# One set of hand-written instruction orders for another in a fused long-convolution and token-MLP kernel

## The chip, the core and the metric

The kernel runs on one core of one Trainium2 chip. The time is that of one execution on the device, in microseconds (us), from repeated runs of the same program; lower is better. The core has five engines, each with its own queue of instructions that it works through in order: TensorE (PE in the profile; PEld is its loading of weights), VectorE (DVE), ScalarE (ACT), GpSimd (POOL) and SyncE (SP, which here only issues DMAs). Engines wait for each other on semaphores.

## The reference, cut to what matters

All tensors are bf16. S = 2048 positions, D = 448 channels, F = 1792.

```python
def _A_ref(q, k, v, shift_k, ssm_k, ssm_D):
    # k_shift: a causal convolution of k with 4 taps (shift_k)
    kv = k_shift * v
    # y: a causal convolution of kv with the filter ssm_k, over all 2048 positions, by FFTs of length 4096
    y = y + kv * ssm_D[None, None, :]
    return q * y

def _B_ref(x, w1, b1, w2, b2):
    h = _layernorm(x, axis=-1)
    u = jnp.einsum("bsd,sf->bdf", h, w1) + b1
    u = _gelu(u)
    y = jnp.einsum("bdf,fs->bds", u, w2) + b2
    return (lambda x, *d: x.transpose(*d))(y, 0, 2, 1)

x = A_q
h = x + _A_ref(_layernorm(x, axis=-1), A_k, A_v, A_shift_k, A_ssm_k, A_ssm_D)
h2 = h + _B_ref(_layernorm(h, axis=-1), B_w1, B_b1, B_w2, B_b2)
return h2
```

So: a short convolution of k, times v; a long convolution with the filter; a gate by the normalised x; then a normalisation and an MLP that mixes positions.

## The kernel before, in words

Position s is written as 16 q + r: q is the partition (128 of them), r one of 16 **row blocks**. The long convolution is a Fourier transform in two stages of matmuls, a product, and two inverse stages. The work is written as steps; each has a name, and the number behind the dot counts the parts of a step, the number behind the colon the instructions of a part (`k1.8:0-7` are eight matmuls, `k1.8:8` what follows them). All line numbers are those of the kernel before.

- `tables` makes the sine tables on the chip: iotas and small products on GpSimd, phases on VectorE (L837 to L844, two halves `tables.6` and `tables.5`), the sine on ScalarE (L847). `tables.4` are small integer sums on VectorE (L822 to L831); `tables.7` makes the tables of the second stage (GpSimd L854, L858, L871; ScalarE L862).
- `loads`, `xload`: DMAs of the filter, k, v and x on SyncE.
- `kT` transposes the filter on TensorE (L1037) and `kv.1` to `kv.8` transpose k (L965); VectorE or ScalarE copies each result out of PSUM (L741 on VectorE, L738 on ScalarE). `kv.9` to `kv.16` are the short convolution on TensorE (L991) and the product with v on VectorE (L1006).
- `k1` and `u1` are the first stage for the filter and for kv (L1058), 16 parts each; every part has an evacuation of 128x896 out of PSUM by ScalarE or VectorE (L1066, L1068), and every second one three DMAs that shuffle partitions, two on GpSimd and one on SyncE (L1074).
- `k2` and `u2` are the second stage (L1093), 16 parts of four matmuls each, and an evacuation for each pair half (L738, L739, L741, L742). A part of `k2` reads what the shuffles of four parts of `k1` wrote: `k2.12` those of `k1.1`, `k1.5`, `k1.9` and `k1.13`.
- `i1` are the products on VectorE (L1160, 16 of them, `i1.15:0` the last), the first inverse stage on TensorE (L1177), evacuations, and copies to the place of the second inverse stage (L1188 and L1201, "inverse copies"; those of row blocks 14 and 15 are separate small ones). `ct0` and `ct` transpose sine tables (L1107) for the second inverse stage.
- `q` and `xn` are the statistics of x (L1237 and L1239 on VectorE, the inverse root on GpSimd) and the normalised x of the first four row blocks (L1270, L1272).
- `i2` is the second inverse stage, one row block r after another (L1303, L1309), then the gate (L1319 on ScalarE, L1321 on VectorE), the product with x (L1329, L1339), sums of squares (L1357), the inverse root on GpSimd (L1367 to L1381) and the normalised row block Q (L1388).
- `mlp`: L1435 and L1445 accumulate w1 over the 16 row blocks of Q for 14 groups of features, seven of them in PSUM while row blocks still come; L1425 is the gelu; L1457 multiplies by w2, and L1460 adds and writes.

What sets the order: five strings, one per engine, list all instructions, and a sixth gives each use of PSUM its bank. Nothing else decides. The scheduler only walks these lists to find out who has to wait for whom:

```python
ORDER = {
    "pe": (
...
        for token in ORDER[e].split():
            step, _, span = token.partition(":")
            lo, _, hi = span.partition("-")
            for k in range(int(lo), int(hi or lo) + 1):
                q.append(steps[step][k])
```

An engine whose next instruction waits does nothing in the meantime, whatever stands behind it.

Of the kernel before, what the change touches and what calls it, by code (L numbers as in the profile page):

```python
# [36 lines left out]
    ),  # L37
    "act": (
# [9 lines left out]
    ),  # L48
    "dve": (
# [14 lines left out]
    ),  # L64
    "pool": (
# [14 lines left out]
    ),  # L80
# [1439 lines left out]
```

## Time and profile before

| what | value |
|---|---|
| time, median of 3 runs (lowest, highest) | 170.63 us (170.56, 170.69) |
| the profiled execution: its own time, its span | 170.65 us, 168.8 us |
| TensorE clock granted in it | 1.000 |
| GpSimd busy | 58.4 us |
| DMA moved | 35.15 MB, mean 208 GB/s |

The span runs from the first to the last instruction of the profiled execution; 1.85 us of its time lie outside. "Busy" counts the time in which an engine executes; matmuls overlap each other, and a busy TensorE is not TensorE at its peak. A row of a timeline gives start, length, engine, line, operation, output and input, count, and in brackets how long the engine was idle ahead of it and what ended that. A row by stretches gives the stretch and its length, then for each engine the busy time and the number of instructions.

### The profile page before, as it was taken

The page shows a single profiled execution, that of the slowest core. Times are in us where ns is not written, and L with a number is a line of the kernel's source. Part 1 is how long each engine was busy: PE and PEld are TensorE (multiplying, and loading weights), DVE is VectorE, ACT ScalarE, POOL GpSimd, SP SyncE. Part 2 cuts the span into 40 slices and gives each one's busy share as a digit, 9 for nine tenths or more (in the row PEclk, how much of TensorE's full clock was granted, in tenths as well). Part 3 has the DMA queues.
Part 4 walks back from the last instruction along what each step waited for, and adds up shares of the span by engine and source line. Part 5 has one row for each costly group of instructions (what it writes and reads, how often), then busy time and mean ns, then how long its engine had stood idle before and what let it go on. Part 6 is the DMA issues. An engine that isn't in the chain of part 4 may idle for free.

```text
span 168.8 us, 3562 instructions
## 1 busy us (share of the span) xinstructions
PE 160.0 (95%) x1416; PEld 93.3 (55%) x1416; DVE 101.9 (60%) x191; ACT 90.4 (54%) x130; POOL 58.4 (35%) x155
## 2 busy tenths in 40 slices
PE   6999999989899989879999999999999999999994
PEld 2787755453333333334554555555577777777783
DVE  7988999999999999999987440000003213132231
ACT  3599848979999999999685803103550000000000
POOL 8345727694830555675777330000000000000000
DMA  5999898893758766748999999930000111101111
GB/s 161 407 308 385 270 290 327 329 362 126 222 134 318 248 195 186 208 135 273 388 398 403 424 420 422 415 129 0 0 0 9 50 54 54 54 2 56 54 54 54
DMA packets 15564, 35.15 MB, mean 208 GB/s; under 512 B 3804, under 2 KB 9644, under 8 KB 15548
## 3 DMA queue, kind: packets, MB, share of 16 engines
q1 hardware_dynamic: 12396, 28.26, 46.1%
q0 software_dynamic: 3008, 6.58, 12.1%
q8 instruction: 11, 0.18, 0.5%
q10 hardware_dynamic: 144, 0.08, 0.2%
q14 instruction: 5, 0.04, 0.1%
HBM read 22.05 MB, written 1.84 MB: 141 GB/s over the span
## 4 chain that ended last, share of the span: by engine, by line
PE 70%; ACT 14%; DMA 5%; DVE 5%; issue 2%; POOL 2%; SPq 0%; DVEq 0%; ACTq 0%
PE ps L1457 25%; PE ps L1435 13%; PE ps L1445 13%; ACT arena L738 7%; DMA arena<-arena 5%; ACT arena L739 4%; PE ps L1309 3%; PE ps L965 3%; ACT arena L1068 3%; PE ps L1024 3%; PE ps L1058 3%; PE ps L1037 3%; DVE arena L1160 2%; POOL arena L1074 2%; PE ps L991 2%
## 5 line engine op out<-in xcount | busy, mean ns | idle before, releaser
L1460 DVE SCALAR_TENSOR_TENSOR arena<-ps,arena 128x448 bf16<-128x448 f32 (+2 forms) x17 | 11.1, 656 | 55.8 <-PE ps L1457 55.8
L1457 PE MATMUL ps<-arena 128*128 128x448 bf16 (+2 forms) x238 | 42.7, 342 | 0.0
L1457 PEld LDWEIGHTS ps<-arena 128*128 128x128 bf16 x238 | 33.3, 145 | 9.5
L1435 PE MATMUL ps<-arena 128*128 128x448 bf16 x112 | 23.5, 353 | 0.0
L738 ACT CAST arena<-ps 128x896 bf16<-128x896 f32 (+1 forms) x29 | 23.1, 933 | 0.0
L1068 ACT CAST arena<-ps 128x896 bf16<-128x896 f32 x24 | 20.2, 919 | 4.1 <-PE ps L1058 3.6
L1445 PE MATMUL ps<-arena 128*128 128x448 bf16 x112 | 22.3, 352 | 0.0
L1074 POOL DMA_DIRECT2D arena<-arena x32 | 17.6, 556 | 7.9 <-ACT arena L1068 7.7
L1425 ACT ACTIVATE arena<-ps,arena 128x448 bf16<-128x448 f32 x14 | 8.2, 632 | 19.3 <-PE ps L1445 10.3
L1093 PE MATMUL ps<-arena 128*64 128x448 bf16 x128 | 15.3, 361 | 1.8 <-ACT arena L739 0.9
L1435 PEld LDWEIGHTS ps<-arena 128*128 128x128 bf16 x112 | 10.7, 98 | 10.6 <-DVE arena L1388 1.1
L1445 PEld LDWEIGHTS ps<-arena 128*128 128x128 bf16 x112 | 11.0, 98 | 10.2
L1160 DVE TENSOR_TENSOR arena<-arena 128x1792 bf16<-128x1792 bf16 x16 | 16.5, 1083 | 0.0
L1177 PE MATMUL ps<-arena 64*128 64x448 bf16 x128 | 14.1, 351 | 1.1 <-ACT arena L738 0.5
L1058 PE MATMUL ps<-arena 128*32 128x448 bf16 x256 | 14.5, 355 | 0.5 <-ACT arena L1068 0.3
L1201 POOL DMA_DIRECT2D arena<-arena x16 | 9.3, 585 | 13.9 <-ACT arena L738 13.0
L1093 PEld LDWEIGHTS ps<-arena 128*64 128x64 f16 x128 | 5.5, 108 | 10.7 <-ACT arena L739 3.4
L1177 PEld LDWEIGHTS ps<-arena 64*128 64x128 f16 x128 | 5.2, 94 | 9.8 <-DVE arena L1160 3.1
L1388 DVE TENSOR_SCALAR arena<-arena 128x448 bf16<-128x448 f32 x16 | 7.6, 509 | 4.8 <-POOL arena L1381 4.8
L1058 PEld LDWEIGHTS ps<-arena 128*32 128x32 f16 x256 | 5.2, 95 | 7.7 <-ACT arena L1068 2.6
L1237 DVE BATCH_NORM_STATS2 arena<-arena 128x6 f32<-128x448 bf16 x16 | 9.4, 613 | 0.0
L739 ACT ACTIVATE arena<-ps 128x896 bf16<-128x896 f32 x10 | 8.6, 926 | 1.1 <-PE ps L1093 1.1
(99 smaller groups left out, 190.4 us busy)
## 6 DMA issues: line engine op xcount, KB each, us to landing
arena<-in_B_w_dram SPq DMA_DIRECT2D x8, 896.0 KB, 9.9
arena<-in_B_w_dram SPq DMA_DIRECT2D x2, 2048.0 KB, 17.3
arena<-arena SPq DMA_DIRECT2D x16, 224.0 KB, 3.8
arena<-arena POOLq DMA_DIRECT2D x32, 112.0 KB, 3.6
arena<-in_B_w_dram SPq DMA_DIRECT2D x2, 1536.0 KB, 18.8
arena<-arena POOLq DMA_DIRECT2D x13, 196.0 KB, 3.8
arena<-in_A_k_dram SPq DMA_DIRECT2D x4, 448.0 KB, 5.8
arena<-in_A_v_dram SPq DMA_DIRECT2D x4, 448.0 KB, 9.2
```

Source lines behind the costliest of these rows:

```text
L738: return e.copy(out=dst(), in_=src())
L739: return e.activation(out=dst(), in_=src(), func=ACT.Copy, scale=scale)
L1058: op("pe", lambda e, W, b=b, r=r, q=q, x=x, c0=c0: e.matmul(PS[32 * q:32 * q + 32, b.slots[x], 0:D], E[:, 2 * r + x, c0:c0 + 32], src[:, r ...
L1068: return e.copy(out=dst, in_=Ppair(b)) if W == "act" else e.tensor_copy(out=dst, in_=Ppair(b))
L1074: shuf[tag].append(op(q_, lambda e, W, g=g, i=i, a=a, nu=nu, jh=jh: e.dma_start(T[a + i:a + i + 4 * nu - 3:4].rearrange("p (j k) c d -> p ...
L1093: op("pe", lambda e, W, b=bs[h], h=h, j=j, c=c, par=par: e.matmul(PS[64 * par:64 * par + 64, b.slots[c], 0:D], FW[:, 64 * c:64 * c + 64], ...
L1160: op("dve", lambda e, W, m=m, i=i: e.tensor_tensor(out=MR(m.slots[0]).rearrange("p (x y) d -> p x y d", x=2), in0=TU[:, i].unsqueeze(2).br ...
L1177: k = op("pe", lambda e, W, b=bs[h], m=ms[h], par=par, t=t, tab=tab, xy=xy, P=P: e.matmul(Pb(b, par), tab[P, :], MR(m.slots[0])[P, xy, :], ...
L1435: op("pe", lambda e, W, r=r, fc=fc, b=bs[fc]: e.matmul(Pb(b), W1A[:, r, 128 * fc:128 * fc + 128], Q[:, r, :], start=(r == 0), stop=(r == R ...
L1445: op("pe", lambda e, W, r=r, fc=fc, b=b: e.matmul(Pb(b), W1B[:, r, 128 * (fc - n0):128 * (fc - n0) + 128], Q[:, r, :], start=(r == 0), sto ...
L1457: op("pe", lambda e, W, r=r, fc=fc, b=b, d0=d0, d1=d1: e.matmul(Pb(b)[:, d0:d1], W2[fc // 7][:, fc % 7, r:S:R], G[:, fc, d0:d1], start=(fc ...
L1460: op("dve", lambda e, W, r=r, b=b, A=A, d0=d0, d1=d1: e.scalar_tensor_tensor(out=XR(r)[:, d0:d1], in0=Pb(b)[:, d0:d1], scalar=bm[:, r:r + ...
```

## The change

The strings of all five engines and that of the PSUM banks are replaced by others. The operations are the same, with the same operands; 1416 matmuls, 16 products and all DMAs are still there, and the code that builds them is untouched (it stands 8 lines further down). Some evacuations go from ScalarE to VectorE and some back, which the same strings decide. The tokens of one place on VectorE and one on SyncE:

```diff
     "dve": (
-        "dummy.0:0 tables.3:0-1 kv.0:3 tables.6:0 tables.4:16 tables.5:0 tables.4:17 tables.6:1 tables.4:18 "
+        "dummy.0:0 tables.5:0 tables.3:0 tables.5:1 tables.3:1 tables.5:2 tables.6:0 kv.0:3 tables.6:1 kv.5:8 "
...
     "sp": (
-        "loads.6:0 loads.8:0 loads.0:0 loads.1:0 loads.2:0 loads.3:0 loads.13:1 loads.14:0 loads.14:1 loads.10:0 "
+        "loads.8:0 loads.0:0 loads.6:0 loads.2:0 loads.3:0 loads.1:0 loads.4:1 loads.4:0 loads.14:1 loads.4:2 "
```

**The start, ScalarE.** The first rows of its queue before: the sine's table and a first sine on one element, three copies of transposed k, the two halves of the sine table, the copy of `ct0`, and then stage one.

```order
L785 ACT_TABLE_LOAD
L785 ACTIVATE arena<-arena 128x1
L738 COPY arena<-ps 128x2x4x128 x3
L847 ACTIVATE arena<-arena 128x2048 x2
L738 COPY arena<-ps 128x1024
L738 CAST arena<-ps 128x14
L862 ACTIVATE arena<-arena 128x384
L1068 CAST arena<-ps 128x896 x20
```

And now (lines are 8 higher):

```order
L746 ACT_TABLE_LOAD
L746 COPY arena<-ps 128x2x4x128
L855 ACT_TABLE_LOAD
L855 ACTIVATE arena<-arena 128x2048
L793 ACTIVATE arena<-arena 128x1
L855 ACTIVATE arena<-arena 128x2048
L746 COPY arena<-ps 128x8x128
L746 COPY arena<-ps 128x8x64 x2
L746 COPY arena<-ps 128x8x128
L1076 CAST arena<-ps 128x896 x2
```

One copy of k (`kv.6:12`) stands ahead of the sine, and a table load on each side of it; four copies of the transposed filter follow, which VectorE made before.

**The start, TensorE.** Its queue behind the first fillers: L965 transposes k, L1037 the filter, L1024 are fillers, L1107 is `ct0.0`, which reads the first sine table, and L1058 is stage one. Before:

```order
L965 MATMUL ps<-arena 128x128 x8
L1037 MATMUL ps<-arena 128x128 x12
L1024 MATMUL ps<-arena 128x448 x3
L1037 MATMUL ps<-arena 128x128 x16
L1024 MATMUL ps<-arena 128x448 x3
L1037 MATMUL ps<-arena 128x128 x12
L1107 MATMUL ps<-arena 128x128 x8
L1037 MATMUL ps<-arena 128x64 x16
```

And now:

```order
L1045 MATMUL ps<-arena 128x128 x12
L1032 MATMUL ps<-arena 128x448 x3
L973 MATMUL ps<-arena 128x128 x4
L973 MATMUL ps<-arena 64x128 x8
L973 MATMUL ps<-arena 128x128 x8
L1115 MATMUL ps<-arena 128x128 x8
L1045 MATMUL ps<-arena 128x128 x20
L1045 MATMUL ps<-arena 128x64 x16
L1045 MATMUL ps<-arena 128x128 x16
```

`ct0.0` stood behind 40 transposes of the filter and now stands behind 12.

**The middle, GpSimd.** Its queue around the tables of the second stage; L1074 (now L1082) are the shuffle copies of stage one, L854, L858, L871 and L874 make the tables. Before, the tables stand ahead of all copies:

```order
L854 TENSOR_SCALAR arena<-arena 128x128 x3
L858 TENSOR_TENSOR arena<-arena 128x384
L871 TENSOR_TENSOR arena<-arena 128x128 x3
L874 TENSOR_SCALAR arena<-arena 128x128
L943 CAST arena<-arena 128x16
L1074 DMA arena<-arena 8x4x1792 x26
```

And now, behind the first seven copies:

```order
L1082 DMA arena<-arena 8x4x1792
L862 TENSOR_SCALAR arena<-arena 128x128
L1082 DMA arena<-arena 8x4x1792
L801 IOTA arena 128x128
L862 TENSOR_SCALAR arena<-arena 128x128 x2
L814 IOTA arena 128x16
L1253 TENSOR_SCALAR arena<-arena 128x2
L814 IOTA arena 128x128
L1082 DMA arena<-arena 8x4x1792
L866 TENSOR_TENSOR arena<-arena 128x384
L1082 DMA arena<-arena 8x4x1792 x10
L879 TENSOR_TENSOR arena<-arena 128x128
```

The tables and their iotas stand among the copies; `k1.1:9` is the eighth of the ten in the last row but one.

**Elsewhere.** On VectorE one statistic of x and three small instructions move behind the last product. k's second stage begins on TensorE between parts of `u1` (`k2.12` behind `u1.12`), where before it began with `k2.0` ahead of `u1.10`. On SyncE the copies `i1.14:20` and `i1.14:22` come earlier, and seven small copies (`i1.1`, `i1.6`, `i1.10`, `i1.12`) come behind `i1.16:19-20`, among the loads of w1. On TensorE the matmuls of the MLP that take the row blocks one by one are mixed more finely. The gates of row blocks 8 and 13 go from VectorE to ScalarE.

174 rows, old and new, of tables (ORDER, SLOTS) are left out of this document.

## The prediction

> **What bounds the kernel now.** I read the page first, then the chain of work that ended last in order of time, then busy time by stretches, then the timelines of single engines.
>
> ```profile
> span 168.8 us, 3562 instructions
> PE 160.0 (95%) x1416; PEld 93.3 (55%) x1416; DVE 101.9 (60%) x191; ACT 90.4 (54%) x130; POOL 58.4 (35%) x155
> ```
>
> TensorE is busy 95% of the span, VectorE and ScalarE a good half. That is a mean over two parts, and the chain of work shows where one hands over to the other:
>
> ```profile
> 67.89 0.99 DVE arena L1160
> 68.92 0.95 PE ps L1177 x8
> 69.89 0.91 ACT arena L738
> 70.82 0.67 SPq L1188
> 71.55 3.99 DMA arena<-arena
> 75.58 2.82 PE ps L1309 x14
> ...
> 96.05 7.19 PE ps L1435 x38
> ```
>
> The last product on VectorE (`i1.15:0`, ended at 68.88) releases the last matmuls of the first inverse stage, their evacuation ends at 70.80, the copies of it land at 75.54, and from 75.58 on the chain is TensorE alone, at 7.19 / 38 = 0.189 us for a matmul, without a hole to speak of. So the end is **T0** = 75.58 plus a rest bound by TensorE, which can hardly become shorter. What sets T0 is seen by stretches (time, then busy time and instructions of PE, PEld, DVE, ACT and POOL):
>
> ```profile
> 14.00:35.00 21.00, 20.09 (x435) 11.86 (x436) 19.84 (x31) 16.93 (x21) 13.64 (x27) 1.00 0.91 319
> 35.00:50.00 15.00, 13.75 (x164) 5.65 (x160) 14.48 (x24) 13.92 (x18) 9.70 (x21) 1.00 0.62 204
> 50.00:69.00 19.00, 17.68 (x160) 6.29 (x160) 18.75 (x24) 19.00 (x25) 7.60 (x13) 1.00 0.74 232
> ```
>
> All three engines are nearly full: VectorE is idle for 1.16 + 0.52 + 0.25 = 1.9 us of these 55, TensorE for 3.5, ScalarE for 5.2. VectorE is the tightest, so I count on VectorE: when it starts, what it has to do, and its holes.
>
> **Part 1, the start: +0.8 us.** The rows of before, of ScalarE, of VectorE, and of TensorE from the chain:
>
> ```profile
> 0.72 1.28 ACT L785 ACT_TABLE_LOAD   x1 [0.72 <-PEq L1505]
> 5.95 2.89 ACT L738 COPY arena<-ps 128x1024 bf16<-128x1024 bf16 x3 [3.46 <-PE ps L965]
> 8.73 3.91 ACT L847 ACTIVATE arena<-arena 128x2048 f16<-128x2048 int32 x2
> 95.75 1.28 ACT L1425 ACT_TABLE_LOAD   x1
> ```
>
> ```profile
> 0.89 0.43 DVE L1016 MEMSET arena<- 128x448 bf16 x1 [0.89 <-PEq L1505]
> 1.55 0.34 DVE L810 TENSOR_SCALAR arena<-arena 128x128 bf16<-128x128 int32 x1 [0.23 <-POOL arena L789]
> 8.72 0.69 DVE L741 COPY arena<-ps 128x1024 bf16<-128x1024 bf16 x1 [0.29 <-PE ps L1037]
> 9.79 1.29 DVE L741 COPY arena<-ps 128x1024 bf16<-128x1024 bf16 x2 [0.19 <-PE ps L1037]
> 11.46 2.72 DVE L741 COPY arena<-ps 128x1024 bf16<-128x1024 bf16 x5
> 15.35 1.09 DVE L1068 CAST arena<-ps 128x896 bf16<-128x896 f32 x1 [0.49 <-PE ps L1058]
> ```
>
> ```profile
> 4.92 3.26 PE ps L965 x38
> 8.18 0.75 PE ps L1037 x12
> 8.93 0.57 PE ps L1024 x3
> ```
>
> Before, the sine's table is loaded at 0.72, when ScalarE has nothing else. Now an evacuation stands first, with a table of its own, and the sine's load behind it. The first transposes still end at 5.95, the copy takes to 6.96, the load to 8.25, the first sine (3.91 / 2 = 1.95) to 10.25. TensorE does the same 40 transposes of k, 12 of the filter and three fillers first, 4.92 + 3.26 + 0.75 + 0.57 = 9.50, and then comes to `ct0.0`, which transposes that sine table and was later before: it stands 0.75 us, and VectorE, which copies what TensorE transposes, stands with it. VectorE's holes up to its first stage-one evacuation: before 0.89 + 0.23 + 0.29 + 0.19 + 0.49 and 0.1 of crumbs = 2.2; now 0.89, 0.4 (the phase product waits for the row iota), 0.6 ahead of `kv.3`, 0.7 ahead of `ct0.0`, 0.35 behind the next transposes, my estimate from the times above = 2.95. Hence +0.8. Ends: 0, if the load is hidden in the wait for the transposes, and +2.2.
>
> [...] The row at 95.75 shows 1.28 us. [...]
>
> **Part 2, VectorE's work up to the last product: +0.9 us.**
>
> ```profile
> 43.44 3.10 DVE L742 TENSOR_SCALAR arena<-ps 128x896 bf16<-128x896 f32 x3
> 49.91 10.22 DVE L1160 TENSOR_TENSOR arena<-arena 128x1792 bf16<-128x1792 bf16 x10
> 68.78 2.20 DVE L1237 BATCH_NORM_STATS2 arena<-arena 128x6 f32<-128x448 bf16 x4
> 47.84 14.72 ACT L738 CAST arena<-ps 128x896 bf16<-128x896 f32 x18
> ```
>
> Back to back, an evacuation of 128x896 takes VectorE 1.0 us (3.10 / 3) and ScalarE 0.8 (14.72 / 18), a statistic 0.53; a copy of 1024 elements 0.6 and of 512 0.35 (three and two of them make the 2.72 above); an aggregate about 0.1. Counted in the two orders up to `i1.15:0`, VectorE gains two evacuations of k2 and two of u2 and loses one of i1 (+3.0), gains the copy of `ct0` (+0.6), loses four filter copies (-1.9), one statistic (-0.5) and three small ones (-0.3): +0.9. ScalarE, up to its last evacuation of i1, loses three evacuations (-2.4) and `ct0` (-0.9) and gains the four filter copies (+2.8), one normalisation (+0.7) and the load (+1.3): +1.5, which its 5.2 us of holes cover; uncovered, it costs those 1.5. The table sums on VectorE, 0.1 each, only change place: nothing.
>
> **Part 3, the holes between: as before, 0 us.** The change puts GpSimd's table work among the shuffle copies of stage one.
>
> ```profile
> 7.41 2.03 POOL L854 TENSOR_SCALAR arena<-arena 128x128 int32<-128x128 int32 x3 [2.67 <-DVE arena L831]
> 9.53 1.02 POOL L858 TENSOR_TENSOR arena<-arena 128x384 int32<-128x384 int32 x1
> 32.22 5.39 POOL L1074 DMA_DIRECT2D arena<-arena  x10 [1.38 <-ACT arena L1068]
> 30.30 4.45 DMA arena<-arena
> ```
>
> Before, 2.03 + 1.02 lie in GpSimd's idle time. Now they, and 1 us of iotas, stand with 12 copies at 0.54 ahead of the copy `k1.1:9`: 10.5 us from the copies of `k1.15` on, whose evacuation I put at 24.4, so issue at 34.9. k's second stage, moved forward, begins with `k2.12` and needs that copy; landing some 4 us later (4.45 in the last row) is 38 to 39, while TensorE gets there about 37.3. This stand takes the place of the one before (TensorE behind that last row, 34.75), and VectorE then has evacuations of u1 and a statistic to go on with. So I carry the 1.9 us over. Ends: -1.9 (no holes) and +1.5 (the whole stand on top).
>
> **Part 4, behind T0: +0.3 us.** Each later row block of the second inverse stage waits for the gate (L1319, L1321) of the block ahead of it.
>
> ```profile
> 76.18 1.48 ACT L1319 ACTIVATE arena<-ps,arena 128x448 f32<-128x448 f32 x2 [0.56 <-PE ps L1309]
> 77.56 0.56 ACT L1357 ACTIVATE arena<-arena 128x448 bf16<-128x448 f32 x1
> 78.12 0.71 ACT L1319 ACTIVATE arena<-ps,arena 128x448 f32<-128x448 f32 x1
> 78.41 0.68 DVE L1321 TENSOR_SCALAR arena<-ps,arena 128x448 f32<-128x448 f32 x1
> 75.60:100.00 24.40, 24.40 (x128) 12.21 (x129) 19.23 (x57) 16.30 (x39) 14.91 (x39) 1.00 0.99 376
> DMA to landing us min/median/max: 11.1/13.1/13.5
> ```
>
> Block 8's gate, at 78.41 on VectorE, is now ScalarE's fifth piece, behind gate, gate, gate and square: on the old clock 76.18 + 0.76 + 0.76 + 0.62 + 0.56 + 0.72 = 79.6, where TensorE is ready after 20 matmuls, at 79.35. Then block 1's normalised rows come about 0.15 late, and block 9's gate, two pieces further on, 0.3. Together 0.7 of standing, against 0.2 in the trace of before; and one filler matmul (0.19) now lies in the wait ahead of T0: +0.3. Ends: -0.2 (gates as early as before) and +1.5 (each of six later gates 0.2 late). The statistics moved back have room: VectorE is busy 19.23 of 24.40 us there, and gives two gates to ScalarE.
>
> On SyncE the copies that set T0 (`i1.16:19-20`) stay right behind their evacuation. Seven small copies, which only row blocks 14 and 15 need, now stand behind them among the loads of w1. The last lands about 12 us behind T0 if it takes what the loads of w1's second half take (last row). Block 14 is multiplied after 70 matmuls, at T0 + 13.9 with the standing. Covered by 2 us; uncovered, 1 to 2.
>
> **The sum.** 0.8 + 0.9 + 0 + 0.3 = +2.0 on the profiled execution's 170.65 us (its span of 168.8 and 1.85 around it; the median of the runs shown is 170.63): 172.6.
>
> **Rivals.** (a) *The holes close*: with PSUM's slots dealt anew and free statistics as fillers, VectorE has no hole from 14 to 69 us, and the table load is hidden: 0 + 0.9 - 1.9 + 0.3 = -0.7, 170.0. Slower becomes faster where more than 2.0 us are saved at the start and in the holes. For it, the many short waits of before; against it, that they are only 1.9. Chance 0.2. (b) *GpSimd's queue*: the stand at `k2.12` is not covered, +1.5: 174.1. For it, TensorE takes its work in a fixed order; chance 0.15. (c) *The first sine is later still*, by 1.4 us, and nothing can be done meanwhile: 174.0; for it, the engine's load now has a consumer right behind; chance 0.1. [...] (d) *The parts cancel*: just so much hole closes as is added, 170.6; chance 0.08. (e) The forecast, 171.0 to 173.6: 0.47.
>
> **How the numbers follow.** 0.2% is 0.34 us, about what a measurement of this kernel can tell from no change. Faster is (a), 0.2; same is (d), 0.08; slower all others, 0.72. Half of (a) lies below 169.9, the far parts of (b) and (c) above 174.6, together 0.2: the range is 169.9 to 174.6.
>
> **What would show it.** Right: two table loads on ScalarE, the second near 7 us; a hole of TensorE ahead of L1115 near 10 us; the last L1168 ending near 70.6; the dense L1317 x14 starting near 77.3; and from there a chain of TensorE with less than 1 us of waits. Wrong: an end of L1168 before 69 makes (a); a wait of L1101 for a DMA near 38 us with VectorE idle too makes (b); a gap over 1 us between load and sine (c); a wait of the last L1317 pairs for a DMA, the copies on SyncE.

## The result and the profile after

| | before | after |
|---|---|---|
| time, median (lowest, highest), 4 runs each | 170.61 us (170.56, 170.69) | 176.61 us (175.43, 177.79) |
| the profiled execution: its own time, its span | 170.65, 168.8 us | 175.43, 173.6 us |
| ratio after to before | | 1.035, 95% interval 1.026 to 1.044 |

The change makes the kernel 3.5% slower. Its four runs fall into two pairs: 175.43 and 175.65 us at a granted TensorE clock of 1.00, 177.57 and 177.79 us at a mean of 0.99; the profile is one of the first pair. So there are two questions: where 4.8 us come from at the full clock, and what costs 2.1 us more in the other pair.

The page of the changed kernel (its lines are 8 higher than those of before):

```profile
span 173.6 us, 3566 instructions
PE 159.0 (92%) x1416; PEld 92.3 (53%) x1416; DVE 101.6 (59%) x188; ACT 92.9 (54%) x134; POOL 61.4 (35%) x155
```

TensorE has the same 1416 matmuls and about the same busy time, in a span 4.8 us longer: the loss is all standing. The chain of work that ended last (start, length, what):

```profile
68.57 2.02 DVE arena L1168 x2
...
70.63 0.95 PE ps L1185 x8
...
73.26 3.66 DMA arena<-arena
...
77.08 0.55 PE ps L1317 x2
...
88.03 1.39 POOL arena L1256
89.43 0.69 DVE arena L1329
...
96.84 1.40 POOL arena L1389 x2
...
100.38 1.37 DVE arena L1396 x3
...
101.79 0.55 PE ps L1443 x2
```

T0, the start of the long run of matmuls of the second inverse stage (the expectations below call it the first dense i2), is at 77.08 instead of 75.58: +1.50. Before, the chain was TensorE alone from there on. Now it runs over GpSimd and VectorE until 101.79, and TensorE stands for them. Its timeline at the four largest stands behind T0 (the bracket is the idle time ahead, and what ended it):

```profile
84.15 1.69 PE L1443 MATMUL ps<-arena 128*128 128x448 bf16 x8 [0.41 <-DVE arena L1396]
...
90.18 0.55 PE L1317 MATMUL ps<-arena 128*128 128x448 bf16 x2 [0.74 <-DVE arena L1329]
...
96.62 0.35 PE L1453 MATMUL ps<-arena 128*128 128x448 bf16 x1
98.17 0.36 PE L1443 MATMUL ps<-arena 128*128 128x448 bf16 x1 [1.20 <-DVE arena L1396]
...
101.79 0.55 PE L1443 MATMUL ps<-arena 128*128 128x448 bf16 x2 [0.23 <-DVE arena L1396]
```

I count a stand from start to start, less the 0.189 us of a matmul: 98.17 - 96.62 - 0.189 = 1.36 us ahead of `mlp.10:0`. In the same way it is 0.57 ahead of `mlp.2:2`, 0.91 ahead of `i2.84`, 0.40 ahead of `mlp.13:5`. Over all matmuls behind T0 this **lost time** is 3.65 us; before it was 0.20. One matmul fewer lies behind T0 (-0.19). Together 1.50 + 3.46 - 0.19 = 4.77 us, the whole difference of the two profiled executions (4.78). In other profiles at the full clock with the same first part (e4, e6 to e9, e12) T0 lies between 77.02 and 77.95, so the 1.50 holds for this execution, and a difference of a few tenths up to T0 can't be read from one profile.

Where the 1.50 us up to T0 come from, by stretches (PE, PEld, DVE, ACT, POOL; the second stretch ends with the last product). Before:

```profile
0.00:14.00 14.00, 12.63 (x132) 9.19 (x135) 12.29 (x26) 9.54 (x10) 7.22 (x47) 1.00 0.89 299
14.00:68.86 54.86, 51.44 (x753) 23.71 (x752) 52.94 (x77) 49.71 (x61) 30.95 (x60) 1.00 0.77 258
```

After:

```profile
0.00:14.00 14.00, 11.30 (x126) 8.18 (x127) 11.09 (x18) 9.61 (x10) 3.06 (x36) 1.00 0.89 295
14.00:70.57 56.57, 51.10 (x755) 24.09 (x753) 54.55 (x83) 51.52 (x63) 35.09 (x72) 1.00 0.74 245
```

VectorE is idle 2.91 us of the first 14 instead of 1.71 (+1.2), then 2.02 instead of 1.92 (+0.1), and its work up to the last product is 65.64 instead of 65.23 (+0.4): the product ends 1.7 us later. From there to T0 it is 6.51 instead of 6.72 us.

### The profile page after: what moved, and what is told of

Same layout as the page of the kernel before. It is cut to its first block, busy times and chain, and to the rows that moved or that the text cites. A ratio compares the mean times of both kernels' runs of the same rounds, so it can differ in the third digit from the quotient of the medians.

```text
span 173.6 us, 3566 instructions
## 1 busy us (share of the span) xinstructions
PE 159.0 (92%) x1416; PEld 92.3 (53%) x1416; DVE 101.6 (59%) x188; ACT 92.9 (54%) x134; POOL 61.4 (35%) x155
## 3 DMA queue, kind: packets, MB, share of 16 engines
HBM read 22.05 MB, written 1.84 MB: 138 GB/s over the span
## 4 chain that ended last, share of the span: by engine, by line
PE 53%; POOL 14%; ACT 10%; DVE 9%; DMA 7%; issue 5%; POOLq 0%; DVEq 0%; SPq 0%
PE ps L1465 24%; PE ps L1453 11%; DMA arena<-arena 7%; ACT arena L746 5%; PE ps L1443 4%; DVE arena L1168 4%; POOL arena L1082 4%; PE ps L1066 2%; POOL arena L1389 2%; PE ps L1032 2%; PE ps L1045 2%; DVE arena L749 2%; PE ps L999 2%; PE ps L973 2%; POOL arena L1385 2%
## 5 line engine op out<-in xcount | busy, mean ns | idle before, releaser
L1443 PE MATMUL ps<-arena 128*128 128x448 bf16 x112 | 26.6, 353 | 1.9 <-DVE arena L1396 1.8
L1453 PE MATMUL ps<-arena 128*128 128x448 bf16 x112 | 25.1, 352 | 0.0
L746 ACT CAST arena<-ps 128x896 bf16<-128x896 f32 (+1 forms) x28 | 22.6, 920 | 1.2 <-PE ps L1101 0.6
L1082 POOL DMA_DIRECT2D arena<-arena x32 | 18.1, 571 | 9.1 <-ACT arena L1076 8.8
L1209 POOL DMA_DIRECT2D arena<-arena x16 | 9.5, 595 | 13.2 <-ACT arena L746 11.9
L746 ACT COPY arena<-ps 128x1024 bf16<-128x1024 bf16 (+2 forms) x10 | 8.9, 930 | 3.7 <-PE ps L973 3.3
L1014 DVE TENSOR_TENSOR arena<-ps,arena 128x512 bf16<-128x512 f32 (+1 forms) x16 | 9.2, 611 | 0.4 <-PE ps L999 0.4
L1317 PE MATMUL ps<-arena 128*128 128x448 bf16 x32 | 7.6, 353 | 2.0 <-DMA arena<-arena 1.2
```

The lines of the kernel that those rows point to most:

```text
L746: return e.copy(out=dst(), in_=src())
L1082: shuf[tag].append(op(q_, lambda e, W, g=g, i=i, a=a, nu=nu, jh=jh: e.dma_start(T[a + i:a + i + 4 * nu - 3:4].rearrange("p (j k) c d -> p ...
L1209: op(q_, lambda e, W, j=j, p0=p0, a=a, b_=b_, j0=j0: e.dma_start(TZ[p0:p0 + 29:4, j0:j0 + (b_ - a) // 8].rearrange("p r c d -> p r (c d)") ...
L1443: op("pe", lambda e, W, r=r, fc=fc, b=bs[fc]: e.matmul(Pb(b), W1A[:, r, 128 * fc:128 * fc + 128], Q[:, r, :], start=(r == 0), stop=(r == R ...
L1453: op("pe", lambda e, W, r=r, fc=fc, b=b: e.matmul(Pb(b), W1B[:, r, 128 * (fc - n0):128 * (fc - n0) + 128], Q[:, r, :], start=(r == 0), sto ...
```

## The experiments

The time is in us. "Lost" is TensorE's lost time behind T0 in the profiled execution. Line numbers differ by a few between the kernels.

| run | edit | runs at clock 1.00 (0.998 and 0.999 too) | runs at 0.99 and below | lost |
|---|---|---|---|---|
| e1 | changed kernel's first part, tail of before | 172.31, 172.84 | 174.64, 175.66 | 1.1 |
| e2 | first part of before, changed tail | 173.33 to 174.00 (4) | none | 3.5 |
| e3 | TensorE's tail alone from before | none | 181.32 to 184.30 (4) | 7.5 |
| e4 | the other engines' tails from before | 176.38, 177.52, 177.61 | 179.16 | 5.2 |
| e5 | `k1.1` shuffles forward | 174.71 to 175.19 (4) | none | 3.6 |
| e6 | `q.8` forward | 175.00, 176.04 | 177.64, 177.67 | 3.4 |
| e7 | e6, and row block 10 forward | 175.02, 175.32, 176.29 | 178.02 | 3.0 |
| e8 | variance chain on VectorE | 174.95, 174.97, 175.84 | 176.51 | 3.2 |
| e9 | TensorE asks later | 172.94, 173.34, 173.51 | 175.41 | 1.2 |
| e10 | first table early | 174.68, 174.74, 176.03 | 176.05 | 4.1 |
| e11 | e5, e9 and e10 | 171.85, 172.41, 173.00 | 172.75 | 1.6 |
| e12 | none, changed kernel again | 175.64, 175.65, 176.43 | 177.55 | 3.5 |
| e13 | before, `k1.1:9` later | none | 173.58 to 175.78 (4) | |
| e14 | before, `k1.1:9` later still | none | 176.03 to 177.28 (4) | |
| e15 | changed kernel, `k1.1:9` later | none | 179.55 to 181.94 (4) | |
| e16 | e5 and e9 | 172.64 to 173.83 (4) | none | |

All 28 runs of the kernel before beside them were at 1.00 or 0.999, from 170.02 to 171.54 us.

### Which half of the order costs what

**e1** joins the two kernels behind the last `i1` of every engine; **e2** is the converse. At the joint on TensorE, e1:

```diff
 i1.16:10-17 i1.16:1-8
-warm.0:0 ct.1:0-7 ct.2:0-7 i2.1:0-3 i2.9:0-3 ct.0:0-7
+ct.0:0-7 warm.0:0 i2.1:0-3 ct.1:0-7 i2.9:0-3
```

> Every engine's order, and the PSUM banks, of the changed kernel up to the last instruction of i1, and of the kernel before behind it. Theory A (the two parts add up: the order up to the last product costs 1.5 us, the order behind it 3.3 us): about 172.2 us, with the first dense i2 matmul near 77.1 and under 0.6 us of lost time of TensorE behind it. Rival B (the first part leaves VectorE and GpSimd late, and that is what the rows behind it pay for): 174.5 to 175.5 us, with the waits behind the first dense i2 as in the changed kernel. On the second mode of the changed kernel (granted clock 0.99 and 2.2 us more in two of its four runs): if it comes from the first part's order, some of these runs show it too.

> The other half: the orders of the kernel before up to the last instruction of i1, those of the changed kernel behind it. Theory A: about 173.8 us, with about 3.2 us of lost time of TensorE behind the first dense i2. Rival B: 171 us at most. On the second mode: if it comes from the order behind i1, some of these runs show a granted clock of 0.99 and about 176 us.

At the full clock e1 gave 172.31 and 172.84, e2 173.33 to 174.00: the two costs add up in the times, as theory A has it. The profile of e1 is of its run at 175.66, at the low clock, so its T0 (79.72) and its 1.1 us lost, more than the 0.6 foretold, are no test of A. In e2 the product ends at 69.14, 1.4 us earlier than in the changed kernel, and TensorE's timeline behind T0 has the same stands all the same:

```profile
88.72 0.55 PE L1311 MATMUL ps<-arena 128*128 128x448 bf16 x2 [0.74 <-DVE arena L1323]
...
96.70 0.36 PE L1437 MATMUL ps<-arena 128*128 128x448 bf16 x1 [1.19 <-DVE arena L1390]
...
100.33 0.55 PE L1437 MATMUL ps<-arena 128*128 128x448 bf16 x2 [0.23 <-DVE arena L1390]
```

So the 3.5 us belong to the order behind the products, whatever comes ahead. The low clock showed in two of four runs of e1 and in none of e2, which points to the first part; e5 and e13 to e15 below test it.

### What makes TensorE stand behind T0

**e3** and **e4** split the tail by engine. e3 takes TensorE's:

```diff
 i2.45:0-1
-i2.28:0-1 i2.17:0-1 i2.32:0-1 i2.20:0-1 i2.41:0-1 i2.54:0-1 mlp.0:2 mlp.0:1 mlp.0:3-4
+i2.17:0-1 i2.41:0-1 i2.20:0-1 i2.54:0-1 i2.28:0-1 i2.32:0-1 warm.1:0 mlp.0:2-6
```

> The changed kernel, but TensorE's order behind the last i1 (and the PSUM banks and ScalarE's order of gelus that belong to it) from the kernel before; VectorE, GpSimd and ScalarE's i2 as in the changed kernel. Theory C (TensorE takes rows 10 to 15 too early, the rows themselves are hardly later): 172.5 us, since all but the 0.9 ahead of i2.84 and 0.6 at row block 2 are gone or covered. Theory D (GpSimd and VectorE finish the rows late, whoever asks): 173.5 to 175.5 us, with stands of TensorE at row 10's Q, which ends 21 us behind the first dense i2 where the kernel before has it at 17.7.

> The converse: the changed kernel with TensorE's own order, but the orders of VectorE, GpSimd and ScalarE behind the last i1 from the kernel before (statistics of x forward, q.8:5 ahead of i2.49:2, row 10's chain ahead of those of rows 12 and 14). Theory C: TensorE still asks too early, 174 us or more. Theory D: the rows are ready earlier, 172.0 to 173.0 us, and the stands at i2.84 and mlp.10:0 are under 0.3 us each.

e3 is far above either theory: TensorE waits for gates and copies that ScalarE does in another order, and all its runs are at a low clock (about 2.9 of its 7.5 us lost are matmuls that took 0.37 us instead of 0.19).

```profile
78.58 1.67 PE L1297 MATMUL ps<-arena 128*128 128x448 bf16 x4 [2.66 <-ACT arena L732]
...
89.17 2.05 PE L1429 MATMUL ps<-arena 128*128 128x448 bf16 x5 [3.21 <-ACT arena L1313]
```

e4 is no clearer. Its time is within theory C's "174 us or more", yet the stands at `i2.84` and `mlp.10:0` are gone, as theory D has it; 2.1 us are lost among the first matmuls of row block 0 and 1.5 ahead of `mlp.12:5`. A tail is one set of orders; half of one against half of another does not decide between C and D.

**e6** undoes the move of the last statistics, **e7** also brings row block 10 ahead of 12 and 13 on GpSimd:

```diff
 "dve"
+q.8:0 q.8:3 q.8:1 q.8:4
 i2.26:0 i2.27:0 i2.43:0
-q.8:0
 i2.56:0
-q.8:3 q.8:1
 i2.39:0
-q.8:4
 "pool"
+q.8:5
 i2.49:0-2 i2.50:0
-q.8:5
```

```diff
 "pool"
-i2.75:1 i2.88:0 i2.75:2 i2.0:0 i2.88:1 i2.76:0 i2.88:2 i2.89:0 i2.77:0
+i2.0:0 i2.75:1-2 i2.76:0 i2.77:0 i2.88:0-2 i2.89:0
```

> The changed kernel with the last statistics of x (q.8:0, 8:3, 8:1, 8:4) ahead of i2.26 on VectorE and the inverse root q.8:5 ahead of i2.49:0 on GpSimd. Theory (moved back, q.8:5 comes 0.9 us late for the gate of row block 12): the 0.91 us hole ahead of i2.84 goes, 174.5 us in the mode at clock 1.00 (175.5 now). Rival: GpSimd's chain is the limit as a whole, and what the gate gains is lost at row blocks 6 and 10 (q.8:5 pushes i2.49 back by its 1.4 us): 175.3 us or more. A few runs may show the 0.99 clock as in the changed kernel.

> The edit before, and on GpSimd the chain of row blocks 10 and 11 (i2.0, i2.75:1, i2.75:2, i2.76, i2.77) ahead of i2.88 of row blocks 12 and 13. Theory: row 10's Q ends over 1 us earlier, the 1.36 us hole ahead of mlp.10:0 goes to under 0.3: 173.2 to 173.5 us at clock 1.00. Rival: row blocks 12 and 13 are late instead and TensorE stands there for as long: within 0.3 us of the run without this edit.

Each edit did what it says and gained almost nothing. In e6 the 0.91 ahead of `i2.84` is gone, but 0.5 stand ahead of `mlp.6:5`, and lost is 3.4. In e7 the 1.36 ahead of `mlp.10:0` is gone, and the last stand has grown to as much, here by TensorE's timeline of e7:

```profile
101.38 0.55 PE L1440 MATMUL ps<-arena 128*128 128x448 bf16 x2 [1.35 <-DVE arena L1393]
```

Both rivals fit, though one run of e6 (175.00) is just under its rival's bound: what one row block gains another pays.

**e8** takes the 28 small instructions off GpSimd, by one word in each of four lines and a place in VectorE's order:

```diff
-                    op("pool", lambda e, W, hs=hs: e.tensor_scalar(out=hs[:, 4:6], in0=hs[:, 0:2], scalar1=1.0 / D,
+                    op("dve", lambda e, W, hs=hs: e.tensor_scalar(out=hs[:, 4:6], in0=hs[:, 0:2], scalar1=1.0 / D,
```

> The changed kernel with the 28 small instructions of the variance of row blocks 2 to 15 (i2.23, i2.24 and their like, all but the inverse root) on VectorE instead of GpSimd, each group ahead of the next VectorE instruction that was there when its sums were ready. Theory (GpSimd's serial chain, which stands behind VectorE's wide instructions, bounds the rows behind the first dense i2): under 1.0 us of lost time of TensorE there in place of 3.65, 172.5 to 173.0 us at clock 1.00. Rival: VectorE has no room for them (28 at about 0.15 us are 4.2 us, its idle time there was 5.8 us): Q ends as late as before, 175 us or more.

The rival again, within 0.05 us. Both stretches begin at T0 (time, then PE, PEld, DVE, ACT, POOL). The changed kernel:

```profile
77.10:101.50 24.40, 21.97 (x111) 10.22 (x111) 18.59 (x57) 17.32 (x41) 17.93 (x39) 1.00 0.99 370
```

e8:

```profile
77.90:102.30 24.40, 22.34 (x113) 10.21 (x113) 23.10 (x86) 17.32 (x40) 9.13 (x11) 1.00 0.97 359
```

GpSimd falls from 17.93 to 9.13 us, VectorE rises from 18.59 to 23.10 of 24.40 and is the bound: the rows are no earlier.

**e9** leaves the rows and changes only what TensorE does meanwhile. A matmul whose row block was not ready in the changed kernel's profile stands behind ready ones:

```diff
 mlp.9:4 mlp.9:0-1
-mlp.19:1 mlp.10:0 mlp.19:2-5 mlp.10:1 mlp.9:5 mlp.9:3 mlp.10:5 mlp.7:6 mlp.19:6 mlp.10:4
+mlp.19:1-5 mlp.9:5 mlp.9:3 mlp.19:6-7 mlp.8:6 mlp.19:8 mlp.10:0-1 mlp.10:5 mlp.10:4
```

> The changed kernel with TensorE's order alone rewritten behind the first dense i2: same instructions, same PSUM banks, but a matmul on a row block that is not ready by the profile of the changed kernel stands behind one that is (mlp.19:2 to 19:8, mlp.9:5 and the like ahead of mlp.10:0, mlp.12 before mlp.13, mlp.5:4, 5:3 and 5:0 ahead of i2.84). Theory C2 (the rows are about 1 us later, and most of the loss is that TensorE asks for them 2 to 4 us before, with ready work behind): the lost time behind the first dense i2 falls from 3.65 to about 1.4 us, 173.1 us at clock 1.00 (175.3 in the other mode, which this edit leaves). Theory D (the rows are late, and whatever order TensorE has, it must wait for them): lost 3 us or more, 174.8 to 175.5 us.

172.94 to 173.51 us at the full clock and 1.24 us lost: theory C2 held. By the stretch from T0, VectorE and GpSimd do exactly what they did; TensorE alone does more:

```profile
77.04:101.44 24.40, 23.74 (x123) 11.29 (x124) 18.59 (x57) 17.23 (x41) 17.93 (x39) 1.00 0.98 350
```

So of the 3.46 us, 2.4 are TensorE's order against these rows: it asks for a row block before it is there, with ready matmuls queued behind. The other 1.0 goes, by their times, with rows that come later (block 2's Q ends 7.0 us behind T0 instead of 6.1, block 6's 13.5 instead of 12.5); no run takes it by itself.

### The start, and the clock

**e10** puts the first sine's table back at the head of ScalarE, **e5** brings two shuffle copies forward on GpSimd:

```diff
 "act"
-kv.6:12 tables.5:3 tables.0:5 tables.6:3
+tables.0:5 kv.6:12 tables.5:3 tables.6:3
```

```diff
 "pool"
+k1.1:9-10
 u1.3:9
-k1.1:10
 u1.3:10 u1.1:9-10
-k1.1:9
 u1.7:9
```

> The changed kernel with tables.0:5 back at the head of ScalarE's order, so that the copy kv.6:12 stands behind it and no second table load stands ahead of the first sine. Theory of the prediction's part 1: the first sine and ct0.0 come 0.8 to 1.3 us earlier, TensorE's hole of 1.32 us ahead of ct0.0 goes, and the last product ends 0.8 us earlier: 174.6 us at clock 1.00. Rival: the stand at k2.12 and VectorE's evacuations take it up, and the last product moves by less than 0.3 us.

> The changed kernel with one edit: the two shuffle copies k1.1:9 and k1.1:10 are issued on GpSimd ahead of the copies of u1.3 and u1.1 (2.2 us earlier for k1.1:9). Theory: TensorE's stand ahead of k2.12 (1.73 us in the profile of the changed kernel, 2.3 us in the first experiment, where the granted clock then was 0.50 for 3 us) is the wait for k1.1:9; without it the stand is under 0.6 us, and every run has the granted clock 1.00, so the second mode (2.2 us) is gone: about 174.5 to 175.3 us in every run. Rival: the second mode has another origin (the hole at the start, or those behind the first dense i2): half the runs stay at 0.99 and 177 us. Rival: VectorE's evacuations, not the copy, are the limit up to 50 us: the stand moves to the next k2 parts and the fast mode stays at 175.5 us.

In e10 the second load and TensorE's hole are gone, `ct0.0` starts at 8.92 instead of 9.67, and the last product ends at 70.27 instead of 70.57: 0.3 us, near the rival. But this profile is of the run at 176.03; the other two at the full clock, 174.68 and 174.74, are in the theory's time and have no profile. With the first part unchanged the product ends anywhere from 70.44 to 71.25 (the changed kernel, e4, e6 to e9, e12), so e10 does not decide. Its stand ahead of `k2.12` is still there, 1.89 us. The stand in the changed kernel, and in e5 the same place, on TensorE's timelines:

```profile
38.54 0.95 PE L1101 MATMUL ps<-arena 128*64 128x448 bf16 x8 [1.73 <-DMA arena<-arena]
```

```profile
37.56 0.95 PE L1098 MATMUL ps<-arena 128*64 128x448 bf16 x8
```

e5 has no stand there and no run below the full clock, in the time expected; the gain at the full clock is about 0.6 us. What the low clock is shows in the profile of e1, which was taken in such a run (columns as above; the last but two is the granted clock):

```profile
37.00:38.00 1.00, 0.17 (x4) 0.00 (x0) 1.00 (x2) 0.70 (x2) 1.00 (x3) 1.00 0.89 204
38.00:39.00 1.00, 0.00 (x0) 0.00 (x0) 0.70 (x2) 0.46 (x1) 1.00 (x3) 1.00 0.89 319
39.00:40.00 1.00, 0.48 (x4) 0.34 (x6) 0.00 (x0) 0.00 (x0) 0.98 (x3) 0.56 0.94 256
40.00:41.00 1.00, 1.00 (x8) 0.28 (x4) 0.00 (x0) 0.00 (x0) 0.68 (x2) 0.50 0.77 158
41.00:42.00 1.00, 1.00 (x14) 0.42 (x16) 0.74 (x1) 0.77 (x1) 0.00 (x0) 0.50 0.99 330
42.00:43.00 1.00, 1.00 (x20) 0.29 (x12) 0.55 (x2) 1.00 (x2) 0.00 (x0) 0.74 1.00 357
```

TensorE stands from 37.17 to 39.52. The clock is at one half from 39.1 to 42.5 us (0.56 and 0.74 are mixtures of 1.00 and 0.50): 3.4 us, in which matmuls take about twice as long (0.37 us instead of 0.19 in e3; here the first eight of `k2.12` 1.70 us instead of 0.95 in the changed kernel), and VectorE and ScalarE, which wait for them, are idle from 39 to 41 us. The stand itself is 0.6 us longer here than in the profile of the changed kernel, so not all of such a run's extra time is the clock's.

**e12** is the changed kernel again; **e13** and **e14** give the kernel before such a stand, **e15** lengthens that of the changed kernel. Each moves `k1.1:9` alone, e13 here:

```diff
 "pool"
 u1.1:9-10
-k1.1:9
 k1.1:10 u1.3:9-10 k1.5:9-10
+k1.1:9
 u1.5:9-10
```

> The changed kernel as it is, for its two modes. Theory: TensorE stands ahead of k2.12 for 1.3 to 2.4 us, by the start of each execution; where it is about 2 us or longer the granted clock halves for 3 us: one or two of four runs at 0.99 and 177.5 us, and a profile of such a run has the low clock between 39 and 44 us. Rival: the low clock lies at another place of the span.

> The kernel before with one edit: the shuffle copy k1.1:9 is issued on GpSimd ahead of u1.5:9, near 32.2 us instead of 27.5, so that it lands near 36 us and TensorE stands about 1.7 us ahead of k2.0. Theory: the stand costs time (up to 1.3 us more than the 0.5 us that stands there already), but leaves the granted clock at 1.00 in most runs: 170.8 to 172.2 us. Rival (the low clock has nothing to do with stands of TensorE): no run below 1.00 here nor in the next one.

> The same with k1.1:9 ahead of k1.7:9, issued near 33.3 us and landing near 37.2: TensorE stands about 2.7 us ahead of k2.0. Theory: the granted clock is 0.99 in all or nearly all runs, with one half of it for 3.4 us from 37 to 41 us on, 173 to 175 us. Rival (the low clock has nothing to do with stands): every run at 1.00, 171 to 173 us.

> The changed kernel with k1.1:9 issued 1.1 us later (behind u1.7:9 and k1.3:10), so that TensorE stands about 2.8 us ahead of k2.12 instead of 1.3 to 2.4. Theory: 0.99 in all or nearly all runs, 177.5 to 178.5 us. Rival: half of the runs as in the changed kernel, 175.5 to 176.5 and 178 us.

All twelve runs of e13 to e15 were at 0.979 to 0.99. All three missed their times, upwards. e13 missed its length too: the copy landed later than I had put it, and TensorE stood 3.67 us, so it is no test of a short stand. In e14 it stood 4.42 us instead of 2.7, and in e14 and e15 the half clock lasted twice as long as in e1. The timeline of e14 has the stand, and its stretches the clock:

```profile
38.39 4.60 PE L1084 MATMUL ps<-arena 128*64 128x448 bf16 x24 [4.42 <-DMA arena<-arena]
```

```profile
34.00:36.00 2.00, 0.00 (x0) 0.00 (x0) 1.29 (x2) 1.58 (x2) 1.71 (x4) 0.99 1.06 266
36.00:38.00 2.00, 0.00 (x0) 0.00 (x0) 0.00 (x0) 0.00 (x0) 2.00 (x4) 0.50 1.00 294
...
42.00:43.00 1.00, 1.00 (x8) 0.26 (x6) 1.00 (x2) 0.55 (x1) 0.54 (x1) 0.61 0.00 0
```

Half clock from 36.0 to 42.8, twice 3.4 us. e12 had one run at 0.99, but its profile is of a run at 1.00, with a stand of 1.84 us: where the clock falls in the changed kernel itself was not seen. It is shown for e1, which has the same first part.

**e11** and **e16** put the edits that gained together:

> The edits of e5 (k1.1 shuffles forward), e9 (TensorE asks later) and e10 (first table early) together on the changed kernel. If they add: e5 gives 0.5 and takes the second mode away, e9 2.3, e10 0.0 to 0.8: 171.9 to 172.7 us, every run at clock 1.00. Rival: rows or holes that one edit leaves take up what another gives: 173.3 us or more.

> The edits of e5 (k1.1 shuffles forward) and e9 (TensorE asks later) on the changed kernel, without that of e10. Theory: 175.0 less 2.3 is 172.5 to 172.8 us, every run at clock 1.00. Rival (the low clock of one run of e11 comes of something that these edits leave): a run at 0.99.

e16 gave 172.64 to 173.83, two of four above what was foretold, all at 1.00; e11 gave 171.85 to 173.00, but one run at 0.99, where none was foretold and its profile, at 1.00, has no stand at `k2.12` (it has one of 1.50 us ahead of `u2.0`). What lowered the clock there is open. That run took 172.75 us, no longer than the others. Neither version beats the kernel before.

## Why the prediction was wrong

The direction was right; 172.6 us was 4.0 below the median and 2.8 below the profiled execution.

**Parts 1 to 3, up to the last product: right in sum, by luck in the terms.** 0.8 + 0.9 + 0 was foretold, 1.2 + 0.4 + 0.1 came: part 1 was half as large again, part 2 less than half its size, and the two misses cancel. In part 1 the hole ahead of `ct0.0` is 1.32 us instead of 0.7: the sine ends at 9.61 where 10.25 was foretold, but TensorE is there at 8.35 already, not at 9.50. The signs were there: ScalarE's timeline has the two loads and, 0.01 us behind the second, the sine.

```profile
0.72 1.28 ACT L746 ACT_TABLE_LOAD   x1 [0.72 <-PEq L1513]
5.29 1.01 ACT L746 COPY arena<-ps 128x1024 bf16<-128x1024 bf16 x1 [3.28 <-PE ps L973]
6.32 1.28 ACT L855 ACT_TABLE_LOAD   x1
7.61 2.00 ACT L855 ACTIVATE arena<-arena 128x2048 f16<-128x2048 int32 x1
```

This settles rival (c). Its 1.4 us, and with them part 1's upper end (0.8 + 1.4 = 2.2), are a term that no run shows: the load takes 1.28 us, starts 0.02 us behind the copy, and the sine starts 0.01 us behind it. The trace of before has the like: the load at 95.75 starts 0.02 us behind the instruction ahead of it, and behind the one at 0.72 to 2.00 the first sine begins at 2.29.

```profile
2.29 0.20 ACT L785 ACTIVATE arena<-arena 128x1 bf16<-128x1 f32 x1 [0.29 <-POOL arena L784]
...
95.54 0.19 ACT L1357 ACTIVATION_READ_ACCUMULATOR arena<-arena 128x1 f32 x1
```

What the load alone is worth at the last product stays open: 0.3 us in the profile of e10, but two of its three runs at the full clock are 1.3 us shorter than the profiled one.

**Part 3, the stand at `k2.12`: its price at the full clock was right, its second price was missing.** The stand came near 38 us as foretold, with VectorE idle beside it, and VectorE's idle time from 14 us to the last product still grew by only 0.1. Rival (b)'s sign, a wait for a DMA near 38 us with VectorE idle too, was there; its price, 1.5 us, was not. What I had not priced is that the stand can cost 3.4 us of half clock: +2.1 in two of the four runs, and so about half of that in the median. e5 and e16, without the stand, had none in eight runs (e11, without it too, one in four); e13 to e15, with 2.9 us or more in their profiles, had it in twelve of twelve.

**Part 4, behind T0: the step that failed.** It put +0.3 with an upper end of +1.5; 3.3 came (3.46 lost, less 0.19). It counted two gates and the rows of block 1, and then took TensorE's matmuls as always ready. Two things have no term in it at all. TensorE's finer mix of the MLP comes to row blocks 11 to 15 after 1.5 to 4.0 us less of its own matmuls (to block 15 after 22.5 us of them, before after 26.5); and GpSimd's new order mixes block 10's chain with that of block 12, so that its Q ends 21.0 us behind T0 instead of 17.7 (19.1 in e7, which undoes the mixing), where TensorE asks for it after 17.8 us of matmuls as ever. With ready matmuls put ahead of both, e9 got 2.4 us back. The sentence "The statistics moved back have room: VectorE is busy 19.23 of 24.40" looked at the wrong engine: behind the last statistic stands an inverse root on GpSimd, which now stands behind block 6's chain (`i2.49`, `i2.50`) in a queue without room. The timeline of GpSimd:

```profile
86.93 0.42 POOL L1380 TENSOR_TENSOR arena<-arena 128x2 f32<-128x2 f32 x1
87.44 0.51 POOL L1385 TENSOR_SCALAR arena<-arena 128x2 f32<-128x2 f32 x1
88.03 1.38 POOL L1256 TENSOR_TENSOR arena<-arena 128x4 f32<-128x4 f32 x1
```

The gate of block 12 needs it and starts 12.35 us behind T0 (89.43), before 10.1. e6 shows that to move it forward again is worth little by itself, since the chain is full.

**SyncE's copies** were covered: no stand behind T0 waits for a DMA.

**The range** reached to 174.6 because its upper ends knew neither the 2.4 nor the clock. What stays open: which of the orders makes the rows themselves 1.0 us later, and what lowered the clock in one run of e11.

## What to carry to other kernels

Where one engine is the bound behind a point, list its instructions in their new order against the time at which each one's input is ready in the trace of before: an order that asks early is paid in full, even where ready work stands behind it (2.4 us here, and e9's reorder of TensorE alone got them back). A moved instruction is followed to the engine that takes its result, and that queue's room is counted. And a stand of TensorE can have two prices, its length and 3.4 us at half clock, which came with 2.35 us of standing in e1, with 2.9 us or more in e13 to e15 and behind 1.94 us in e3, and not with 1.95 us in e4 and 2.14 us in e8.

## What the runs showed of the hardware

**The clock.** In e1 it fell to 0.50 at 39.1 us, in a stand of 2.35 us, and came back 3.4 us later; in e14, in a stand of 4.42 us, it came back after 6.8. In e3 it fell 1.0 us after TensorE had gone on from a stand of 1.94 us. In the 3.41 us ahead of the fall TensorE was busy for 1.47 us, in e1 (from 35.70 to 39.11) as in e3 (from 37.03 to 40.44). The three falls of e3, at 40.44, 77.99 and 88.23, are 37.55 and 10.24 us apart, 11 and 3 times 3.41. Eight profiles with stands of 1.24 to 2.14 us ahead of `k2.12` had the full clock: the changed kernel with 1.73 us, and 1.68 us of work in the 3.41 us around it, e4 with 1.95, e8 with 2.14. So neither the length of the stand decides alone nor the work in the 3.41 us around it, which in e8 is at most 3.41 - 2.14 = 1.27 us; what does, these runs do not show.

**GpSimd beside VectorE.** Behind T0 a small instruction of GpSimd (128x2, not the inverse root) takes 0.19 to 0.22 us where VectorE is idle all the while (13 of the 56 in the profiles of before and after), and up to 0.61 beside VectorE. The changed kernel, VectorE and then GpSimd:

```profile
95.20 0.68 DVE L1337 SCALAR_TENSOR_TENSOR arena<-arena 128x448 f32<-128x448 bf16 x1
```

```profile
95.32 0.61 POOL L1378 TENSOR_TENSOR arena<-arena 128x2 f32<-128x2 f32 x1
96.01 0.19 POOL L1385 TENSOR_SCALAR arena<-arena 128x2 f32<-128x2 f32 x1
```

The first begins under a VectorE instruction and ends 0.05 us behind it, at 95.93; the second has VectorE idle. In the profile of the changed kernel nine of the 28 such instructions began under a product of this kind and over 0.15 us ahead of its end, in that of before three of 28; all twelve ended 0.05 to 0.09 us behind it. Together the 28 take 9.98 us instead of 7.15, and GpSimd is busy 17.93 us behind T0 instead of 14.91; no run was made to price the overlap by itself.
